# Gates spread by tiny matmuls, an output weight relayed by column tiles, and a head whose weights come in parts

## The chip, the cores and the metric

The kernel runs on one core of one Trainium2 chip. The metric is device time in microseconds (us) of one execution; before the change the median of three runs is 1026.72 us. The core's engines each work through a queue of their own in order: PE (TensorE, matmuls; PEld is its weight load), DVE (VectorE), ACT (ScalarE), POOL (GpSimd), and SP (SyncE), which here issues every DMA transfer.

## The reference, cut to what matters

Two blocks A and B, equal in form and with weights of their own, read the same x (2048 x 640). Each projects q, k, v, splits them into 32 heads of 20 columns and 4 segments of 512 rows, runs causal softmax attention inside each segment, and adds a read from a memory that has been summed over the earlier segments. A gate per row of x mixes the two blocks.

```python
phi = lambda t: jnp.where(t > 0, t + 1.0, jnp.exp(t))
g = _sigmoid(beta).reshape(1, H, 1, 1)                  # per head
for s in range(N):                                      # N = 4 segments of L = 512
    logits = jnp.einsum("bhqd,bhkd->bhqk", qs, ks) * scale + mask
    a_dot = jnp.einsum("bhqk,bhkd->bhqd", _softmax(logits, axis=-1), vs)
    num = jnp.einsum("bhld,bhde->bhle", pq, M)          # pq = phi(qs)
    den = jnp.einsum("bhld,bhd->bhl", pq, z)[..., None] + 1e-6
    outs.append(g * num / den + (1.0 - g) * a_dot)
    M = M + jnp.einsum("bhld,bhle->bhde", pk, vs)       # pk = phi(ks)
    z = z + jnp.einsum("bhld->bhd", pk)
return o @ wo                                           # o: outs, heads joined
...
g = _sigmoid((x * gate_w).sum(-1, keepdims=True))       # per row of x
return g * a + (1 - g) * b
```

## The kernel before, in words

**Windows and quads.** The work is cut into 8 windows, t = 0 to 7: window t is block t % 2 (A or B) of segment t // 2. Each window has 8 quads of 4 heads, 64 quads in all. A quad has three stages on PE. The S units (L1250) multiply q blocks with keys into PSUM banks, and DVE takes the causal row maximum out of each (L1237, with mx). The maxima are cast (mt, L1261, L1262), transposed on PE (L1275), copied by ACT (mr, L1292) and sent by two small DMAs (L1287) into two extra rows of the quad's q tile. The T units (L1340) then make the transposed logits with the maximum already taken off; ACT exponentiates them (p, L1332) and POOL zeroes the part above the diagonal (L1333). The PV unit (L1362, the whole array) multiplies p with the values. L1208 loads a quad's q and k (qst, kst) from DRAM, where L719 had stored them.

**Matmuls by halves.** Numbers are fp32; products are made of a high and a low part (wh, wl; two row tiles for x), three matmuls per k tile. But for the head, the last products and PV, each matmul uses 64 of the array's 128 rows, and two streams of such matmuls, the two "lanes", run beside each other (L737 for all projections). The head (L785) is the first q and k product, 30 full matmuls over the five k tiles of x. L322 are matmuls on zeros, at the start (`WARM`) and between the head's steps (`IDLE_STEPS`).

**What sets the order.** Nothing is scheduled by the hardware or a compiler: the kernel's own Python keeps a clock for each engine and queue, with a cost for each instruction, and writes instructions in the order in which that clock would have them ready. `put(engine, cost, emit, then, prio)` queues an instruction on A(CT), D(VE), G(pSimd) or S(P); `dma(us, emit, then, prio, lat)` queues a transfer on SP; `later(prio, ...)` offers a small PE unit to be slipped between others. The table `RULES` gives, for a quad number, the order of S and T units and four numbers (span, calm, lag, room) that steer how much other work lies between them. Between the units PE is filled with the window's jobs: q, k, v products, the output products of the window before (job o), and the next window's first products. What stands in an engine's queue behind an instruction that waits, waits too.

**Head.** `stage(i)` fetches the weights of job i into a staging tile (wst), ACT casts the high part (L538), DVE or POOL subtracts for the low part (L540); L575, L565 and L569 do the same for a tile of x. For the first two jobs this is one transfer of 320 KB each. `begin` stages some jobs ahead and calls `relay(b)` for block b's wo.

**Gates.** The gate's logit per row of x comes out of the v product as one extra column: ACT copies it into pg (L1055), four columns per segment. `spread(s)` has ACT copy it in 16 pieces into the layout the output needs (pgt, L629), ACT takes the exponential for both signs (L592), and DVE adds one (L593, in `over_sigmoid`). Then POOL multiplies the row gates with the head gates (gq, L660). `head_gates` does the same once for the two betas (L599, L592, L593), right after the head's loads.

**wo's relay.** wo's rows have to be re-ordered by heads before job o can load them. `relay(b)` does it by DMA from DRAM to DRAM in three stages: L481 writes nat (5 transfers), L474 writes lin (4), L469 writes wop (4). All transfers of a stage are queued at once, and a stage begins when the one before has landed. Job o then loads a column tile of wop into wst (L548).

Of the kernel before, what the change touches and what calls it, by code (L numbers as in the profile page):

```python
# [12 lines left out]
F32 = mybir.dt.float32  # L13
# [29 lines left out]
def tile_gated_mix_infini_attn(  # L43
# [47 lines left out]
        0: "TTSTSTSTSS 1.0 2.38 0.31 4",  # L91
        1: "TSTSTSTSTS 1.001 2.38 0.32 6",
        3: "TTSTSTSTSS 1.018 2.38 0.32 6",
        4: "TSTSTTSTSS 0.97 2.38 0.33 3",
        5: "TSSTTSSTTS 1.028 2.94 0.33 8",
        6: "TTTSTSTSSS 1.0 2.14 0.33 6",
        7: "TSTSTSTSTS 1.0 2.69 0.33 6",
        8: "TTSSTTSSTS 1.0 2.1 0.33 6",
        9: "TTSTSTSTSS 1.0 2.38 0.33 6",
        10: "TSTSTSTSTS 1.0 2.38 0.33 6",  # L100
        11: "TSTSTSTSTS 0.964 2.38 0.31 6",
        12: "TSTSTSTSTS 0.932 2.38 0.31 6",
        13: "TTSTSTSTSS 0.949 2.38 0.31 6",
        14: "STSTSTSTST 0.963 2.38 0.31 3",
        15: "STSTSTSTST 0.963 2.38 0.38 3",
        16: "TSTSTSTSTS 1.0 2.38 0.33 6",
        18: "TSTSTSTSTS 0.962 1.59 0.3 8",
        19: "TSTSTSTSTS 1.0 2.38 0.33 6",
        20: "TSSTTSSTTS 1.0 2.38 0.33 6",
        21: "TSSTTSSTTS 1.0 2.38 0.46 6",  # L110
        22: "TSTSTSTSTS 0.999 2.38 0.46 8",
        23: "STTSSTTSST 1.0 2.14 0.33 6",
        24: "TSTSTSTSTS 1.0 2.38 0.33 3",
        25: "TSTSTTSTSS 1.036 2.32 0.42 6",
        26: "STTSSTTSST 1.075 2.08 0.42 6",
        27: "STTSSTTSST 1.0 2.38 0.32 6",
        28: "SSTSTSTSTT 1.0 2.38 0.32 6",
        29: "STTSSTTSST 1.03 1.75 0.32 3",
        30: "TSSTTSSTTS 0.95 2.51 0.42 6",
        31: "STSTSTSTST 0.962 2.51 0.42 6",  # L120
        32: "STSTSTSTST 0.932 2.51 0.32 6",
        33: "TTSSTTSSTS 1.027 2.38 0.33 4",
        34: "TSTSTSTSTS 0.965 2.38 0.33 6",
        35: "TTTSTSTSSS 0.997 2.38 0.33 6",
        36: "TSTSTSTSTS 0.985 3.27 0.33 6",
        38: "TSTSTSTSTS 0.944 3.27 0.33 6",
# [12 lines left out]
        51: "STTSSTTSST 1.002 2.38 0.33 6",
        52: "TTTSTSTSSS 0.994 2.38 0.33 6",  # L140
        53: "TSTSTSTSTS 1.0 2.38 0.3 6",
        54: "TSTSTSTSTS 1.0 1.89 0.46 6",
        56: "TTSSTTSSTS 1.0 2.38 0.33 6",
        57: "TSTSTSTSTS 0.975 1.47 0.33 6",
        59: "SSTSTSTSTT 1.0 2.38 0.3 6",
        60: "TSTSTSTSTS 1.0 2.38 0.31 6",
# [155 lines left out]

    def small_tiles():
# [20 lines left out]
    WARM = 9  # L324
    IDLE_STEPS = {3: 5, 4: 2}
# [25 lines left out]
    pgt = const.tile([P, 16 * NSEG], F32, name="pgt")  # L351
# [59 lines left out]
    ROWS = (slice(0, 64), slice(64, 128))  # L411
# [47 lines left out]

    def relay(b):  # L460
# [7 lines left out]
        def third(j):  # L468
            dma(1.2, lambda: nc.sync.dma_start(  # L469
                out=wop[b][32 * j:32 * j + 32], in_=lin[b][j].rearrange("(k q) c -> q k c", k=KT)), last, prio=RELAY[b])  # L470

        def second():
            for j in range(4):
                dma(1.2, lambda j=j: nc.sync.dma_start(  # L474
                    out=lin[b][j].rearrange("(u e) c -> u e c", e=DH),
                    in_=nat[b].rearrange("(u j e) c -> j u e c", u=8, j=4)[j]), lambda j=j: third(j), prio=RELAY[b])

        last = then_all(4, there)
        first = then_all(KT, second)
        for m in range(KT):  # L480
            dma(1.2, lambda m=m: nc.sync.dma_start(  # L481
                out=nat[b][:, P * m:P * (m + 1)].rearrange("(k p) c -> p k c", p=P), in_=weights[b]["o"][m]), first, prio=RELAY[b])
# [3 lines left out]
    VK = ((0, 2), (2, 4), (4, 5))  # L486
    staged = set()
    split = {}

    def stage(i):  # L490
# [35 lines left out]

        def got(w):
# [18 lines left out]
            def fetch():  # L546
                src_ = src[m] if kind in "qk" else wop[t % 2][:, :, P * m:P * (m + 1)]
# [7 lines left out]
        wst.want(1, got, prio=i)  # L555
# [34 lines left out]
    def over_sigmoid(out, in_, sign):  # L590

        nc.scalar.activation(out, in_, AF.Exp, scale=-sign)  # L592
        nc.vector.tensor_scalar(out, out, 1.0, None, op0=ALU.add)  # L593

    def head_gates():
# [4 lines left out]

        def over():
            for b in range(2):
                over_sigmoid(gmem[b], gsel[b], 1.0)
                over_sigmoid(gdot[b], gsel[b], -1.0)

        put("D", 0.8, over, prio=6)
# [18 lines left out]
    def spread(s):  # L625

        def some(a):
            for j in range(4):
                nc.scalar.copy(  # L629
                    pgt[32 * j:32 * j + 32, 16 * s + a:16 * s + 16:4], pg[32 * a:32 * a + 32, NB * s:NB * (s + 1)])  # L630

        def over():
            put("D", 0.5, lambda: segment_gate(s), lambda: (gates_ready.add(s), ask_gates()), prio=7)

        left = then_all(4, over)
        for a in range(4):
            put("A", 0.44, lambda a=a: some(a), left, prio=5)

    def segment_gate(s):
        c = slice(16 * s, 16 * (s + 1))  # L640
        for b, sign in ((0, 1.0), (1, -1.0)):
            over_sigmoid(gate[b][:, c], pgt[:, c], sign)
# [123 lines left out]
    def job_head():  # L766
# [3 lines left out]
        while todo:  # L770
            ready_ = [x for x in todo if x[1] in split and (0, x[0]) in xs]
# [861 lines left out]
```

## Time and profile before

| what | value |
|---|---|
| median of 3 runs | 1026.72 us (1025.70 to 1028.92) |
| the profiled execution: its time, its span | 1025.48 us, 1023.8 us |
| granted TensorE clock | 0.999 |
| busy: PE, DVE, POOL, ACT | 1011.4, 742.7, 735.7, 645.8 us |
| DMA: moved, mean rate | 212 MB, 207 GB/s |

How to read it: PE's busy time counts a moment as busy when either lane works, so a lane that stands alone does not show there. A row of the timeline is: start, length, engine, line, operation, tiles, and in brackets the engine's idle time before it with what ended it. A row of the waits is: who waited for whom, the total in us, how often, the longest. A row of the windows is: the stretch, its length, then for each engine the busy us and the number of instructions, then the granted clock, the DMA engines' share and GB/s.

### The profile page before, as it was taken

The page shows a single profiled execution, that of the slowest core. Times are in us where ns is not written, and L with a number is a line of the kernel's source. Part 1 is how long each engine was busy: PE and PEld are TensorE (multiplying, and loading weights), DVE is VectorE, ACT ScalarE, POOL GpSimd, SP SyncE. Part 2 cuts the span into 40 slices and gives each one's busy share as a digit, 9 for nine tenths or more (in the row PEclk, how much of TensorE's full clock was granted, in tenths as well). Part 3 has the DMA queues.
Part 4 walks back from the last instruction along what each step waited for, and adds up shares of the span by engine and source line. Part 5 has one row for each costly group of instructions (what it writes and reads, how often), then busy time and mean ns, then how long its engine had stood idle before and what let it go on. Part 6 is the DMA issues. An engine that isn't in the chain of part 4 may idle for free.

```text
span 1023.8 us, 29705 instructions
## 1 busy us (share of the span) xinstructions
PE 1011.4 (99%) x10612; PEld 843.4 (82%) x10612; DVE 742.7 (73%) x2570; ACT 645.8 (63%) x1420; POOL 735.7 (72%) x1375
## 2 busy tenths in 40 slices
PE   8999999999999999999999999999999999999998
PEld 7988888888788988888877888888878798887885
DVE  4687876678677678676688668786677776878853
ACT  6576666567755476665876547666486556657672
POOL 4565867767486786976858679697686956868684
PEclk9999999999999999999999999999999999999999
DMA  7998988758556666755766457585665766776522
GB/s 257 277 298 259 318 275 297 222 170 259 149 182 179 190 221 188 245 160 151 276 179 215 136 181 235 165 252 152 184 215 176 247 192 198 237 201 204 157 91 99
DMA packets 136158, 212.09 MB, mean 207 GB/s; under 512 B 12549, under 2 KB 48650, under 8 KB 135946
## 3 DMA queue, kind: packets, MB, share of 16 engines
q1 hardware_dynamic: 136010, 210.19, 66.8%
q8 instruction: 84, 1.38, 0.6%
q14 instruction: 64, 0.52, 0.2%
HBM read 135.69 MB, written 83.23 MB: 214 GB/s over the span
## 4 chain that ended last, share of the span: by engine, by line
PE 91%; ACT 3%; DMA 3%; DVE 1%; issue 1%; SPq 0%; POOL 0%; ACTq 0%
PE bank L737 54%; PE bank L1362 13%; PE bank L1340 7%; PE bank L1250 7%; PE bank L830 4%; PE bank L1002 3%; DMA row<-in_xT_dram 1%; ACT p L1332 1%; PE bank L963 1%; DMA kst<-kd 1%; PE bank L785 1%; DMA qst<-mr 1%; ACT pgt L629 0%; PE bank L1179 0%; DVE row L1164 0%
## 5 line engine op out<-in xcount | busy, mean ns | idle before, releaser
L1237 DVE CUSTOM_DVE_ANT_0 bank<-bank,tri 128x384 f32<-128x384 f32 (+3 forms) x1024 | 473.7, 516 | 103.6 <-PE bank L1250 85.7
L737 PE MATMUL bank<-row,wh 64*128 64x512 f32 x2308 | 526.5, 405 | 0.1
L1332 ACT ACTIVATE p<-bank 128x512 f32<-128x512 f32 x538 | 297.6, 601 | 142.7 <-PE bank L1340 109.5
L737 PEld LDWEIGHTS bank<-row,wh 64*128 64x128 f32 x2308 | 328.8, 185 | 19.2 <-issue 3.2
L737 PE MATMUL bank<-row,wl 64*128 64x512 f32 x1154 | 312.7, 399 | 0.0
L1333 POOL TENSOR_SCALAR_AFFINE_SELECT p<-p 128x256 f32<-128x256 f32 (+1 forms) x538 | 193.6, 370 | 97.0 <-ACT p L1332 87.6
L737 PE MATMUL bank<-wvh,row 64*128 64x320 f32 (+1 forms) x1280 | 204.8, 316 | 0.1
L540 POOL TENSOR_TENSOR wl<-wst,wh 128x640 fp32r<-128x640 f32 x115 | 179.5, 1565 | 31.7 <-ACT wh L538 31.1
L737 PEld LDWEIGHTS bank<-row,wl 64*128 64x128 f32 x1154 | 179.8, 185 | 6.5 <-issue 0.8
L1340 PE MATMUL bank<-qst,kst 62*128 62x512 f32 (+3 forms) x1024 | 177.1, 323 | 4.1 <-DVE mx L1237 1.5
L1250 PE MATMUL bank<-kst,qst 60*128 60x384 f32 (+3 forms) x1024 | 176.8, 318 | 1.2 <-ACT p L1332 0.6
L737 PEld LDWEIGHTS bank<-wvh,row 64*128 64x128 f32 x1280 | 164.5, 186 | 4.8 <-issue 1.7
L940 DVE STREAM_TRANSPOSE row<-bank 128x512 f32<-128x512 f32 x112 | 78.1, 707 | 98.8 <-PE bank L1362 71.4
L1362 PE MATMUL bank<-p,vst 128*32 128x384 f32 (+3 forms) x1804 | 144.9, 423 | 0.0
L1237 DVE DVE_READ_ACCUMULATOR2_ANT mx<- 128x1 f32 x1024 | 144.4, 141 | 0.0
L1340 PEld LDWEIGHTS bank<-qst,kst 62*128 62x128 f32 x1024 | 129.9, 186 | 17.3 <-issue 5.1
L1250 PEld LDWEIGHTS bank<-kst,qst 60*128 60x128 f32 x1024 | 130.3, 186 | 12.0 <-issue 2.3
L1362 PEld LDWEIGHTS bank<-p,vst 128*32 128x32 f32 x1804 | 57.7, 110 | 79.7 <-issue 57.0
L737 PE MATMUL bank<-wvl,row 64*128 64x320 f32 (+1 forms) x640 | 117.6, 313 | 0.0
L538 ACT CAST wh<-wst 128x640 fp32r<-128x640 f32 x119 | 86.6, 740 | 32.5 <-PE bank L737 14.8
L737 PEld LDWEIGHTS bank<-wvl,row 64*128 64x128 f32 x640 | 91.4, 186 | 0.5 <-issue 0.2
L1332 ACT ACTIVATE row<-bank 128x512 f32<-128x512 f32 x102 | 56.8, 601 | 52.7 <-PE bank L1340 48.4
(100 smaller groups left out, 1311.5 us busy)
## 6 DMA issues: line engine op xcount, KB each, us to landing
qd<-row SPq DMA_DIRECT2D x120, 256.0 KB
kd<-row SPq DMA_DIRECT2D x120, 256.0 KB
qst<-qd SPq DMA_DIRECT2D x128, 240.0 KB
kst<-kd SPq DMA_DIRECT2D x128, 240.0 KB
wst<-wop SPq DMA_DIRECT2D x40, 320.0 KB
wst<-in_a_wq_dram SPq DMA_DIRECT2D x20, 320.0 KB
wst<-in_a_wk_dram SPq DMA_DIRECT2D x20, 320.0 KB
wst<-in_b_wq_dram SPq DMA_DIRECT2D x20, 320.0 KB
```

Source lines behind the costliest of these rows:

```text
L538: put("A", 0.628, lambda: nc.scalar.copy(wh, w3), lambda: put(lo_eng, lo_cost, lambda: lo.tensor_tensor(out=wl, in0=w3, in1=r32(wh), op=AL ...
L540: lambda: lo.tensor_tensor(out=wl, in0=w3, in1=r32(wh), op=ALU.subtract), end, prio=3), prio=6)
L737: return nc.tensor.matmul(bank_of, lhsT=w[ROWS[half]], rhs=x_[ROWS[half]], start=start, stop=stop)
L830: return nc.tensor.matmul(b, lhsT=w[r], rhs=r32(pqTs[t, half_m[half]][r, :]), start=start, stop=stop)
L940: put("D", 0.635, lambda: nc.vector.transpose(out=z, in_=b), turned, prio=2)
L1002: return nc.tensor.matmul(b[:, :nh * E1], lhsT=r32(pkn[ROWS[half], P * n:P * (n + 1)]), rhs=vst[ROWS[half], n, LO[m] * E1:(HI[m] + 1) * E1 ...
L1237: put("D", w / 960.0 + 0.112, lambda: nc.vector.tensor_tensor_reduce(out=sc[:, off:off + w], in0=sc[:, off:off + w], in1=tri[:, L - w:], s ...
L1250: lane_ops[half].append((cost_r(w), lambda pair=pair, qb=qb, off=off, w=w, r=r, sc=sc: nc.tensor.matmul(sc[:, off:off + w], lhsT=q[r, pair ...
L1332: put("A", 0.493, lambda: nc.scalar.activation(pt, sc, AF.Exp, scale=SCALE), lambda: (bank.give(sc), put("G", 0.156 + 0.118 * len(todo), l ...
L1333: "G", 0.156 + 0.118 * len(todo), lambda: nc.gpsimd.affine_select(out=blocks, in_=blocks, pattern=[[0, len(todo)], [1, P]], base=0, channe ...
L1340: lane_ops[half].append((cost_r(w), lambda pair=pair, kb=kb, off=off, w=w, r=r, sc=sc: nc.tensor.matmul(sc[:, off:off + w], lhsT=k[r, pair ...
L1362: nc.tensor.matmul(po[32 * j:32 * j + 32, P * kb:], lhsT=vst[:, kb, h * E1:h * E1 + 32], rhs=pts[i, n, f][0][:, off:off + w], start=(kb == ...
```

## The change

- **Gates.** `spread` becomes a PE unit: four matmuls of 64 x 128 by 64 x 4 with a 0/1 matrix `pick`, two on each half of the array, spread pg's columns over the partitions in a PSUM bank. ACT takes exponential and adds one (`nc.scalar.add`), for both signs: four ACT instructions per segment. The 16 copies and the two DVE additions per segment go. `head_gates` has its additions on ACT too, and its two loads are asked for when job 4 begins, no longer ahead of the head's end. POOL makes `pick` once with four copies.
- **wo's relay.** nat, lin and wop are laid out by column tiles of 128. The last stage has 20 transfers of 80 KB in place of 4 of 400 KB, and a helper `in_turn` keeps two transfers of the first and second stage and four of the third on the way at a time. A column tile of wop is now contiguous for job o's load.
- **Head.** The first two jobs' weights come, and are split, in two parts (k tiles 0 and 1, then 2 to 4). The head takes a step once its part is there. `WARM` goes from 9 to 7, and the `IDLE_STEPS` (7 matmuls on zeros) go.
- **Order.** The planner's cost of a DMA's issue goes from 0.37 to 0.48 (0.66 in the relay, 0.7 for L1287's), and `RULES` is another table; the order of all instructions follows from these.

```diff
-        0: "TTSTSTSTSS 1.0 2.38 0.31 4",
-        1: "TSTSTSTSTS 1.001 2.38 0.32 6",
...
+        0: "TSTSTSTSTS 0.97 1.02 0.33 6",
+        1: "TSTSTSTSTS 0.958 1.0 0.46 6",
...
-    def dma(us, emit, then=None, prio=5, lat=2.4, some=False):
+    def dma(us, emit, then=None, prio=5, lat=2.4, some=False, iss=0.48):
...
-        put("S", 0.37, emit, issued, prio)
+        put("S", iss, emit, issued, prio)
...
+        for half in range(2):
+            for c in range(2):
+                nc.gpsimd.tensor_copy(
+                    out=pick[ROWS[half], c, :].rearrange("p (j r) -> p j r", r=32),
+                    in_=ident[ROWS[half], None, 64 * half + 32 * c:64 * half + 32 * c + 32].to_broadcast([64, 4, 32]))
...
-    WARM = 9
-    IDLE_STEPS = {3: 5, 4: 2}
+    WARM = 7
...
+    def in_turn(todo, width, then):
+        left = then_all(len(todo), then)
+        todo = deque(todo)
+
+        def one():
+            if todo:
+                us, emit, prio = todo.popleft()
+                dma(us, emit, lambda: (one(), left()), prio=prio, iss=0.66)
+
+        for _ in range(width):
+            one()
...
+        prio = RELAY[b]
+        in_turn([(1.1, lambda m=m: first(m), prio) for m in range(KT)], 2, lambda: in_turn(
+            [(1.3, lambda j=j: second(j), prio) for j in range(4)], 2, lambda: in_turn(
+                [(0.3, lambda m=m, j=j: third(m, j), prio) for m in range(KT) for j in range(4)], 4, there)))
...
+    HEAD_K = ((0, 2), (2, KT))
...
-        nc.vector.tensor_scalar(out, out, 1.0, None, op0=ALU.add)
+        nc.scalar.add(out, out, 1.0)
...
     def spread(s):
-        def some(a):
-            for j in range(4):
-                nc.scalar.copy(
-                    pgt[32 * j:32 * j + 32, 16 * s + a:16 * s + 16:4], pg[32 * a:32 * a + 32, NB * s:NB * (s + 1)])
...
+        b = bank.free.pop(0)
+        ops = [[((LOAD, 0.06, 0.06), lambda a, z, half=half, c=c: nc.tensor.matmul(
+            b[:, 2 * half + c:16:4], lhsT=pick[ROWS[half], c, :], rhs=pg[ROWS[half], NB * s:NB * (s + 1)],
+            start=True, stop=True)) for c in range(2)] for half in range(2)]
...
+        def segment_gate():
+            c = slice(16 * s, 16 * (s + 1))
+            for g, sign in zip(gate, (1.0, -1.0)):
+                over_sigmoid(g[:, c], b[:, :16], sign)
+
+        return split_unit(*ops, lambda: put("A", 0.85, segment_gate, there, prio=3))
...
-            ready_ = [x for x in todo if x[1] in split and (0, x[0]) in xs]
+            ready_ = [x for x in todo if x[::-1] in head_there and (0, x[0]) in xs]
...
-        gates_in = then_all(NB, lambda: spread(t // 2))
+        gates_in = then_all(NB, lambda: later(2, 0.2, lambda: True, lambda: spread(t // 2)))
```

How the order of instructions moves, at three places. First SP's queue at the very start, before and after: wst are the weights' staging tiles, row the tiles of x.

```order
L548 DMA wst_123<-in_a_wq_dram 128x640
L575 DMA row_9_172<-in_xT_dram 128x512
L548 DMA wst_124<-in_a_wk_dram 128x640
L575 DMA row_16_175<-in_xT_dram 128x512
L575 DMA row_21_178<-in_xT_dram 128x512
L575 DMA row_26_181<-in_xT_dram 128x512
L575 DMA row_31_184<-in_xT_dram 128x512
L548 DMA wst_125<-in_a_wq_dram 128x640
L548 DMA wst_126<-in_a_wk_dram 128x640
L1552 DMA beta_185<-in_a_beta_dram 128x32
L1552 DMA beta_186<-in_b_beta_dram 128x32
L522 DMA wst_123<-in_a_wv_dram 128x640
```

```order
L572 DMA wst_131<-in_a_wq_dram 128x256
L625 DMA row_12_182<-in_xT_dram 128x512
L572 DMA wst_132<-in_a_wk_dram 128x256
L625 DMA row_18_185<-in_xT_dram 128x512
L572 DMA wst_131<-in_a_wq_dram 128x384
L572 DMA wst_132<-in_a_wk_dram 128x384
L625 DMA row_25_188<-in_xT_dram 128x512
L625 DMA row_30_191<-in_xT_dram 128x512
L625 DMA row_35_194<-in_xT_dram 128x512
L598 DMA wst_133<-in_a_wq_dram 128x640
L598 DMA wst_134<-in_a_wk_dram 128x640
L1587 DMA gw<-in_gate_w_dram 5x128
```

The second tile of x stands behind 384 KB less of weights and the third behind none less; the loads of beta are gone from here.

Second the gates of segment 1. On DVE before, the two additions stand between the row maxima of two quads:

```order
L1237 ISA bank_116,mx_4402<-bank_116,tri 128x128
L1237 ISA mx_4402 128x1
L593 TENSOR_SCALAR gate_81<-gate_81 128x16
L593 TENSOR_SCALAR gate_82<-gate_82 128x16
L1237 ISA bank_122,mx_4402<-bank_122,tri 128x512
L1237 ISA mx_4402 128x1
```

On ACT after, where all of the gate's elementwise work now is:

```order
L1096 COPY pg<-bank_130 128x1
L1097 COPY vst<-bank_130 128x16x20
L1373 ACTIVATE p_5441_4524<-bank_127 128x512
L1373 ACTIVATE p_5440_4523<-bank_129 128x512
L1373 ACTIVATE p_5498_4562<-bank_125 128x512
L1373 ACTIVATE p_5499_4563<-bank_123 128x512
L642 ACTIVATE gate_81<-bank_127 128x16
L643 ACTIVATE gate_81<-gate_81 128x16
L642 ACTIVATE gate_82<-bank_127 128x16
L643 ACTIVATE gate_82<-gate_82 128x16
L531 CAST wvh<-wst_133 128x2x320
```

And on PE after, where the first half's two tiny matmuls stand among projections and S units:

```order
L781 MATMUL bank_126<-row_3259_2766,wh_137 128x512
L672 MATMUL bank_127<-pg,pick 128x4 x2
L781 MATMUL bank_126<-row_3264_2769,wh_137 128x512
L781 MATMUL bank_129<-row_3253_2762,wh_139 128x512
L781 MATMUL bank_126<-row_3269_2772,wh_137 128x512
L1291 MATMUL bank_125<-kst_77,qst_73 128x384
```

DVE has nothing left to do for the gates; PE now has a row that needs ACT's copy of pg (L1096), with four exponentials on ACT after the last copy and ahead of the gate itself.

Third SP's queue inside block B's relay, before and after:

```order
L1287 DMA qst_72<-mr_144 2x8x128 x2
L548 DMA wst_123<-wop_113 128x5x128
L522 DMA wst_126<-in_b_wv_dram 128x640
L522 DMA wst_124<-in_b_wv_dram 128x640
L522 DMA wst_125<-in_b_wv_dram 128x320
L474 DMA lin_112<-nat_110 8x12800 x4
L1208 DMA qst_75<-qd_90 60x2x512 x2
L1208 DMA kst_79<-kd_98 60x2x512 x2
L469 DMA wop_114<-lin_112 160x1x640
```

```order
L1249 DMA kst_79<-kd_98 60x2x512 x2
L493 DMA wop_4_117<-lin_111 160x1x128
L488 DMA lin_112<-nat_110 40x2560
L763 DMA kd_98<-row_3111_2660 128x512 x2
L763 DMA kd_98<-row_3112_2661 128x512
L763 DMA qd_90<-row_3124_2666 128x512
L1328 DMA qst_73<-mr_153 2x8x128 x2
L763 DMA qd_90<-row_3124_2666 128x512
L763 DMA qd_90<-row_3125_2667 128x512
L598 DMA wst_133<-wop_0_113 128x640
```

Four transfers of 400 KB stood together ahead of a quad's loads; now one stands alone, and block A's last third-stage transfer lies eight rows ahead of the first load of its wop.

More of the change, by code (lines that the diff above doesn't have):

```diff
@@ L103, in tile_gated_mix_infini_attn @@
[L103 to L114, printed above, removed]
@@ L350, in tile_gated_mix_infini_attn @@
     pg = const.tile([P, NSEG * NB], F32, name="pg")
-    pgt = const.tile([P, 16 * NSEG], F32, name="pgt")
+    pick = const.tile([P, 2, P], F32, name="pick")
     qd = [dram.tile([D, 3, L], F32R, name=f"qd{i}") for i in range(8)]
@@ L356, in tile_gated_mix_infini_attn @@
     part = [dram.tile([D, L], F32, name=f"part{s}") for s in range(NSEG)]
-    nat = [dram.tile([D, D], F32, name=f"nat{b}") for b in range(2)]
-    lin = [dram.tile([4, 8 * DH, D], F32, name=f"lin{b}") for b in range(2)]
-    wop = [dram.tile([P, KT, D], F32, name=f"wop{b}") for b in range(2)]
+    nat = [dram.tile([KT, D, P], F32, name=f"nat{b}") for b in range(2)]
+    lin = [dram.tile([4, KT, 8 * DH, P], F32, name=f"lin{b}") for b in range(2)]
+    wop = [[dram.tile([P, KT, P], F32, name=f"wop{b}_{m}") for m in range(KT)] for b in range(2)]
     NBIG, NWST, NWH, SPARE = 42, 4, 4, 2
@@ L466, in there, with first, second, third @@
                 x[1]()
[L468 to L472, printed above, removed]
-            for j in range(4):
[L474 to L482, printed above, removed]
+        def first(m):
+            nc.sync.dma_start(out=nat[b][m].rearrange("(k p) c -> p k c", p=P), in_=weights[b]["o"][m])
+        def second(j):
+            nc.sync.dma_start(
+                out=lin[b][j].rearrange("m (u e) c -> (m u) (e c)", e=DH),
+                in_=nat[b].rearrange("m (u j e) c -> j (m u) (e c)", u=8, j=4)[j])
+        def third(m, j):
+            nc.sync.dma_start(
+                out=wop[b][m][32 * j:32 * j + 32], in_=lin[b][j][m].rearrange("(k q) c -> q k c", k=KT))
+        prio = RELAY[b]
+        in_turn([(1.1, lambda m=m: first(m), prio) for m in range(KT)], 2, lambda: in_turn(
+            [(1.3, lambda j=j: second(j), prio) for j in range(4)], 2, lambda: in_turn(
+                [(0.3, lambda m=m, j=j: third(m, j), prio) for m in range(KT) for j in range(4)], 4, there)))
     RELAY = (150.0, 260.0)
     VK = ((0, 2), (2, 4), (4, 5))
+    HEAD_K = ((0, 2), (2, KT))
+    head_pair, head_parts, head_there = {}, {}, set()
     staged = set()
@@ L525, in stage, with got_head, take, end @@
             return
+        def got_head(w):
+            w3 = w.rearrange("p (k n) -> p k n", n=P)
+            def take(pair):
+                head_pair[i] = pair
+                def end():
+                    wst.give(w)
+                    split[i] = pair
+                done = then_all(len(HEAD_K), end)
+                for a, b in HEAD_K:
+                    head_parts[a, i] = lambda a=a, b=b: part_(a, b, pair, done)
+            def part_(a, b, pair, done):
+                wh, wl = (x[:, a:b, :] for x in pair)
+                def landed():
+                    put("A", 0.1 + 0.106 * (b - a), lambda: nc.scalar.copy(wh, w3[:, a:b, :]), lambda: put(
+                        "D", 0.06 + 0.155 * (b - a), lambda: nc.vector.tensor_tensor(
+                            out=wl, in0=w3[:, a:b, :], in1=r32(wh), op=ALU.subtract), over, prio=3), prio=6)
+                def over():
+                    head_there.update((i, k) for k in range(a, b))
+                    done()
+                dma(0.185 * (b - a), lambda: nc.sync.dma_start(
+                    out=w3[:, a:b, :], in_=weights[t % 2][kind][m][:, a:b, :]), landed, prio=0)
+            whl.want(1, take, prio=i)
         def got(w):
```

146 lines of the change are left out of this document (77 added, 69 removed).

## The prediction

> **What bounds the kernel now.** First the page's busy line, the shares of the chain that ended last, and then the windows, to see where PE stands still.
>
> ```profile
> PE 1011.4 (99%) x10612; PEld 843.4 (82%) x10612; DVE 742.7 (73%) x2570; ACT 645.8 (63%) x1420; POOL 735.7 (72%) x1375
> PE 91%; ACT 3%; DMA 3%; DVE 1%; issue 1%; SPq 0%; POOL 0%; ACTq 0%
> 0.00:10.00 10.00, 7.41 (x22) 4.85 (x22) 3.29 (x5) 4.55 (x6) 7.38 (x18) 1.00 0.77 249
> 100.00:107.00 7.00, 5.91 (x63) 3.71 (x63) 5.09 (x18) 1.96 (x5) 5.74 (x10) 1.00 0.80 292
> 160.00:180.00 20.00, 19.41 (x229) 17.41 (x227) 12.69 (x49) 13.63 (x28) 15.28 (x28) 1.00 0.91 295
> 270.00:280.00 10.00, 8.08 (x61) 5.24 (x58) 7.49 (x20) 8.57 (x25) 5.02 (x11) 1.00 0.43 144
> 400.00:500.00 100.00, 100.00 (x1070) 85.26 (x1071) 69.67 (x245) 64.22 (x136) 78.37 (x141) 1.00 0.62 188
> 530.00:540.00 10.00, 9.59 (x100) 6.70 (x96) 7.33 (x26) 9.19 (x32) 5.73 (x11) 1.00 0.63 197
> 540.00:550.00 10.00, 9.30 (x74) 6.53 (x67) 9.41 (x29) 6.03 (x15) 8.47 (x14) 1.00 0.73 246
> 1010.00:1024.00 14.00, 9.66 (x49) 7.54 (x47) 5.56 (x10) 0.62 (x1) 2.90 (x3) 0.92 0.25 94
> ```
>
> PE is the bound: 91% of the chain, 100.00 of 100 us busy in an undisturbed stretch. So only two things can shorten the run: less on PE, or fewer places where PE starves. PE's idle time is 1023.8 - 1011.4 = 12.4 us. Of it 2.6 lie in the first 10 us, 4.1 after 1010 (13.8 - 9.66), and the rest in few spots: 1.1 at 100 to 107, 0.6 at 160 to 180, 1.9 at 270 to 280, 1.1 at 530 to 550. A lane that stands alone counts as busy, so the true loss is larger, and the number of matmuls bounds it: the undisturbed stretch does 10.7 per us, 270 to 280 does 61, which is 5.7 us' worth: up to 4.3 us lost. 540 to 550 with 74 lost up to 3.1, 530 to 540 with 100 up to 0.7. These are upper ends, since long matmuls make the count small too.
>
> Next the waits and the chain, for what PE waited on in those spots.
>
> ```profile
> DVE gate L593 <- ACT gate L592: 3.4, 3, 2.0
> PE bank L1340 <- DVE mx L1237: 1.5, 1, 1.5
> PE bank L1340 <- DMA qst<-mr: 1.1, 1, 1.1
> ACT pg L1055 <- PE bank L737: 13.0, 6, 4.3
> SPq L719 <- DMA lin<-nat: 7.3, 5, 2.3
> 99.60 6.14 DMA qst<-mr
> ```
>
> ```profile
> 275.24 1.56 POOL L540 TENSOR_TENSOR wl<-wst,wh 128x640 fp32r<-128x640 f32 x1 [0.36 <-ACT wh L538]
> 275.31 1.60 DVE L593 TENSOR_SCALAR gate<-gate 128x16 f32<-128x16 f32 x2 [1.24 <-ACT gate L592]
> 277.62 0.50 PE L1340 MATMUL bank<-qst,kst 62*128 62x512 f32 x2 [1.49 <-DVE mx L1237]
> 539.02 1.47 DVE L593 TENSOR_SCALAR gate<-gate 128x16 f32<-128x16 f32 x2 [2.04 <-ACT gate L592]
> ```
>
> The spots at 270 and 540 are the gates of segments 1 and 2. DVE reaches L593, waits 1.24 and 2.04 us for ACT's exponential, and then needs 1.60 and 1.47 us for two additions of 16 columns, ending with the POOL subtraction that began beside it. Row maxima stand behind it, and PE's next L1340 waits 1.49 us. The spot at 100 is a transfer of 8 KB (qst<-mr) that took 6.14 us to land while wo's relay was on the way; SP's queue, too, waited 7.3 us for lin's transfers.
>
> **The change part by part.**
>
> *Head.* The rows of the start:
>
> ```profile
> 1.52 3.80 PE L322 MATMUL bank<-qst 128*128 128x512 f32 x9 [1.52 <-DVE qst L316]
> 2.18 6.60 DMA row<-in_xT_dram
> 6.51 1.31 PE L322 MATMUL bank<-qst 128*128 128x512 f32 x5
> 9.47 0.50 PE L785 MATMUL bank<-row,wh 128*128 128x512 f32 x1 [0.94 <-ACT row L565]
> 9.47 5.66 PE bank L785 x22
> 11.56 1.54 ACT L538 CAST wh<-wst 128x640 fp32r<-128x640 f32 x2 [0.18 <-DMA wst<-in_a_wq_dram]
> 13.01 1.70 ACT L599 COPY betaq<-beta 32x8 f32<-32x8 f32 x8
> 15.93 0.50 PE L737 MATMUL bank<-row,wh 64*128 64x512 f32 x1
> ```
>
> PE does 6 of the 30 steps and then starves for x's second tile until 9.47; the rest runs at 5.66 / 22 = 0.257 us a step. Now that tile stands behind 384 KB less, about 1.5 us at the first window's 249 GB/s, so 12 steps are done when the third tile arrives: 6 x 0.257 = 1.5 us saved if the third lands when the second did. It stands behind as much as before, so it may land up to 1 us later; on the other side the next weights' cast, at 11.56, allows products from 12.4 on, 3.5 us earlier than 15.93. ACT's beta copies (1.70 us) no longer stand ahead of the value weights' cast. I take -1.8, near the 1.5, with ends -3.5 and -0.5. The removed matmuls on zeros cost nothing now, they fill the waits for x (0.94 us of it idle); the first 9 still end before the first step. Two more transfers on SP delay the next weights by under 1 us, hidden by the same 12 steps. POOL's four copies for pick stand ahead of the masks that the first DVE maxima need, some 20 us later.
>
> *Gates.* ACT's 16 copies per segment and both DVE additions go; two short ACT instructions come in.
>
> ```profile
> L629 ACT COPY pgt<-pg x64: 180/195/199, 36.6 to 787.9; 32x4 f32<-32x4 f32 x64
> L593 DVE TENSOR_SCALAR gate<-gate x8: 163/304/1518, 40.6 to 791.5; 128x16 f32<-128x16 f32 x8
> L861 ACT ACTIVATE fw<-row x48: 221/232/262, 287.6 to 951.4; 128x16 f32<-128x16 f32 x48
> 19.53 0.43 PE L963 MATMUL bank<-ident,row 64*128 64x64 f32 x4
> L963 PE MATMUL bank<-ident,row 64*128 64x64 f32 x240 | 25.9, 226 | 0.0
> L612 PE MATMUL bank<-ident,gw 64*128 64x64 f32 x2 | 0.5, 271 | 0.0
> ```
>
> ACT loses 64 x 0.195 = 12.5 us and gains 8 x 0.232 = 1.9 (L861 is the same form); it is busy 63%, so neither counts by itself. What counts is DVE's blocked queue: it disappears, since DVE has no gate row any more. Worth between the array's idle time there, 1.9 + 1.1 = 3.0 us, and the counts' 4.3 + 3.1 + 0.7 = 8.1. I take -5.0, nearer the idle time, because the lower counts also hold the long matmuls of the memory reads. Added on PE: 16 matmuls with a weight load of 128 columns, like L963's; four of those take 0.43 us, so they follow at (0.43 - 0.23) / 3 = 0.07, where 0.23 is the mean length of one. 16 x 0.07 = 1.1, half of it beside the other lane: +0.6; ends 0 and 16 x 0.27 = 4.3, if each stood alone as L612's do (0.27). New wait: PE's tiny matmuls need ACT's copy of pg, and behind them stands all of PE. ACT's row for that copy waits for PE (13.0 us in 6), not the other way, so ACT takes pg as soon as the product ends: 0 for it, with a rival below.
>
> *Relay.* Same bytes in smaller and fewer transfers at a time. PE lost 1.1 us at 104 and 0.6 at 173, both in the relays: -1.7, with ends -2.0 and +1.0. SP issues 32 transfers more, 0.593 us each by this row:
>
> ```profile
> L469 SPq DMA_DIRECT2D wop<-lin x8: 567/593/1434, 106.7 to 178.7; - x8
> L548 SPq DMA_DIRECT2D wst<-wop x40: 529/570/812, 143.7 to 985.2; - x40
> ```
>
> That is 19 us of SP over more than 100 us, between transfers that wait for their own engines; hidden unless the relay comes late (rival). The Trainium skill, "DMA: Bandwidth & Descriptors", § Bandwidth, says the opposite of what is done here: batch transfers, to 1 MiB where possible, since each has a fixed cost of about 2 us. By it 32 more transfers, four at a time, would make the two relays 16 us longer in all, and the sum would stay, as nothing waits for them within that time.
>
> *Order.* The table moves every unit. Nothing in the trace of before prices that. Counted over both orders, neighbouring matmuls on the same half of the array, which leave the other lane alone, fall from 1392 to 1315; that speaks for a small gain. I take -1.0; ends -4.0 and +3.0, about what the dips in the undisturbed windows could give or take.
>
> *Sum.* -1.8 - 5.0 + 0.6 - 1.7 - 1.0 = -8.9 against the profiled execution's 1025.48: 1016.6. The median of the runs is 1026.72, 1.24 above that execution, so 1017.8.
>
> **The rivals.**
>
> *The waits only move.* What DVE's block hid comes up behind it: at 540 DVE is busy 9.41 of 10 us even so, at 270 ACT 8.57, and either would be the next to be late. Then the gates give the idle time of one spot, 2.0, and the order nothing: -1.8 - 2.0 + 0.6 - 1.7 = -4.9, median 1021.8. Against it: ACT loses 16 x 0.195 = 3.1 us of copies in just that stretch.
>
> *Slower: the relay comes late.* The last stage needs 20 / 4 = 5 rounds, and each waits for landings, at the lowest priority on SP. Before, the first wop transfer was issued at 106.7 and its first reader at 143.7: 37 us. Five rounds fit if one takes under 7.4 us. With landings of 6.14 us as at 99.60 plus the issue behind other transfers it is close; at 9 us a round wo comes 8 us late, SP stands at the load of wop with the quads' loads behind it, and PE stands with it: -8.9 + 2 x 8 = +7.1, median 1034. Against it: fewer bytes on the way at a time should make landings shorter.
>
> *A cold array.* The nine first matmuls took 3.80 us, 0.42 each, the five at 6.51 about 0.24 once the length of the last is taken off: PE began at about half its speed, though the windows grant it 1.00. With 7 warm-ups and no idle steps the head could run slow: 30 steps x (0.42 - 0.23) = 5.7 us, so -8.9 + 5.7 = -3.2, median 1023.5. The Trainium skill, "TensorE: Matmul & The Clock Gate", § Part 1: The HAM clock gate, says so: the array starts at half clock and needs about 3.4 us of sustained activity, and an idle window puts it back. Against the rival: 7 x 0.42 = 2.9 us of warm-up and 12 steps of the head follow each other with less idle time than before, and x's third tile bounds those 12 steps anyway.
>
> *The order is worth more.* With the lower ends of head, gates, and order, -3.5 - 6.5 + 0.6 - 1.7 - 4.0 = -15.1, median 1011.6 and below.
>
> **How the numbers follow.** Chances: forecast 0.62, waits only move 0.17, order worth more 0.09, slower 0.08, cold array 0.04. 0.3% of 1026.72 is 3.1 us, about what a measurement can tell from no change, so faster means below 1023.6. The forecast and the fourth case are faster, 0.71, and two thirds of the second, 0.11: 0.82. The rest of the second and the cold array: same, 0.10. Slower 0.08. The range takes the forecast, most of the fourth case and all of the second: 1009.5 to 1025.5.
>
> **What would show it.** Head right: L737's row begins at 13 to 14.5 us in place of 15.93, and PE is busy over 8.5 of the first 10 us. Gates right: no DVE wait for a gate, and no stretch of 10 us around the gates with PE under 9.7 busy. Relay right: no landing above 4 us of an 8 KB transfer between 60 and 180, and PE idle there under 0.5 us. The forecast is wrong if the windows between the old spots show new dips of 1 us and more, if PE's waits name ACT's pg or a DMA from wop, or if the first L826 rows follow at 0.4 us.

## The result, and the profile after

The changed kernel takes 1010.58 us (median of 4 runs, 1009.80 to 1012.97) against 1026.21 (4 runs) for the kernel before: ratio 0.9848, 95% interval 0.9821 to 0.9876, or 15.6 us less. The forecast was 1017.8 with 1009.5 to 1025.5. The profiled execution took 1012.97 us, the slowest of the four; its span is 1011.3.

First the page's busy line, the shares of the chain and the windows of the spots that the prediction named (columns as before: stretch, length, PE, PEld, DVE, ACT, POOL with counts, granted clock, DMA share, GB/s).

```profile
PE 1001.1 (99%) x10637; PEld 835.3 (83%) x10637; DVE 737.8 (73%) x2558; ACT 640.9 (63%) x1372; POOL 734.8 (73%) x1379
PE 96%; DMA 2%; SPq 1%; DVE 0%; issue 0%; ACT 0%; ACTq 0%
0.00:10.00 10.00, 7.57 (x20) 5.23 (x21) 4.08 (x8) 4.87 (x8) 8.41 (x22) 1.00 0.76 222
100.00:107.00 7.00, 7.00 (x83) 5.82 (x83) 5.85 (x19) 5.95 (x13) 5.94 (x14) 1.00 0.77 286
160.00:180.00 20.00, 19.87 (x242) 17.39 (x239) 12.79 (x47) 16.00 (x32) 15.29 (x25) 1.00 0.96 319
270.00:280.00 10.00, 9.91 (x74) 7.40 (x70) 5.11 (x16) 5.40 (x16) 6.61 (x13) 1.00 0.62 166
540.00:550.00 10.00, 9.93 (x94) 8.87 (x92) 8.19 (x26) 5.21 (x14) 8.06 (x21) 1.00 0.33 115
```

The spots at 104, 270 and 540 are filled; the one at 170 nearly. What PE waits for now, in its waits (who for whom, total us, times, longest; the first is the start and was 1.5 before, too):

```profile
PE bank L328 <- DVE qst L322: 1.5, 1, 1.5
PE bank L1291 <- DVE row L1020: 1.1, 1, 1.1
PE bank L826 <- ACT row L615: 0.9, 2, 0.6
PE bank L657 <- DMA gw<-in_gate_w_dram: 0.8, 1, 0.8
PE bank L1381 <- ACT p L1373: 0.8, 1, 0.8
PE bank L1381 <- DMA qst<-mr: 0.2, 1, 0.2
```

No wait names the gates any more. But PE's idle time explains little of the result: it falls from 12.4 us to 1011.3 - 1001.1 = 10.2. PE is *busy* 10.3 us less, with 25 matmuls more in its records (32 rows of the tiny ones come in, 7 on zeros go). So the gain lies in stretches that count as busy; that a lane stood alone there is the reading, and the counts of matmuls agree with it. A window without gates, relay or head shows it, 600 to 700, first of before and then of after:

```profile
600.00:700.00 100.00, 99.87 (x1054) 81.96 (x1052) 80.64 (x272) 65.55 (x139) 80.61 (x145) 1.00 0.68 209
```

```profile
600.00:700.00 100.00, 100.00 (x1089) 83.48 (x1087) 78.58 (x260) 69.12 (x147) 81.04 (x148) 1.00 0.69 214
```

Both are full, yet the second does 35 matmuls more in the same 100 us. It is the widest gap of the six windows from 300 to 900, which hold 6335 and 6452 matmuls together. To see where the time was won, take one event per quad, the first row of its PV unit in PE's timeline (start, length, line). Quads 12, 28, 44 and 60 of before, then of after:

```profile
231.40 0.62 PE L1362 MATMUL bank<-row,vst 128*32 128x512 f32 x2
...
495.38 1.06 PE L1362 MATMUL bank<-p,vst 128*32 128x512 f32 x8
...
752.46 0.62 PE L1362 MATMUL bank<-row,vst 128*32 128x512 f32 x2
...
976.70 0.62 PE L1362 MATMUL bank<-p,vst 128*32 128x512 f32 x2
```

```profile
232.90 0.62 PE L1403 MATMUL bank<-row,vst 128*32 128x512 f32 x2
...
487.77 1.06 PE L1403 MATMUL bank<-row,vst 128*32 128x512 f32 x8
...
741.20 1.06 PE L1403 MATMUL bank<-p,vst 128*32 128x512 f32 x8
...
962.97 1.07 PE L1403 MATMUL bank<-p,vst 128*32 128x512 f32 x8
```

The differences are +1.5, -7.6, -11.3, -13.7 us. At quad 12 head and both relays are over, and this execution had gained nothing; the gain grows from there to near the end, through gates and quiet stretches alike. Two things limit the reading. The execution had stray waits of 0.8 us at 153 and 1.1 at 180; the kernel with whole head weights (below), whose order is otherwise the same, was profiled at 1010.47 us and has the four events at 230.13, 485.06, 738.38 and 960.34, that is 1.3, 10.3, 14.1 and 16.4 us ahead of the kernel before. And single quads scatter by some us (-7.4 at quad 48, -17.3 at quad 56), since a rule moves a unit against the work around it; only the trend counts.

One correction to the text ahead of the prediction: `IDLE_STEPS` names 7 matmuls, but only the five after step 3 are issued, so the change removes 2 + 5 matmuls on zeros, not 2 + 7 (PE has 14 rows of them before, 7 after).

### The profile page after: what moved, and what is told of

The parts are those of the page before. It is cut to its first block, busy times and chain, and to the rows that moved or that the text cites. A ratio compares the mean times of both kernels' runs of the same rounds, so it can differ in the third digit from the quotient of the medians.

```text
span 1011.3 us, 29724 instructions
## 1 busy us (share of the span) xinstructions
PE 1001.1 (99%) x10637; PEld 835.3 (83%) x10637; DVE 737.8 (73%) x2558; ACT 640.9 (63%) x1372; POOL 734.8 (73%) x1379
## 4 chain that ended last, share of the span: by engine, by line
PE 96%; DMA 2%; SPq 1%; DVE 0%; issue 0%; ACT 0%; ACTq 0%
PE bank L781 57%; PE bank L1403 15%; PE bank L1381 7%; PE bank L1291 7%; PE bank L871 4%; PE bank L1043 3%; PE bank L1004 1%; DMA gw<-in_gate_w_dram 1%; DMA kd<-row 1%; DMA qst<-mr 1%; PE bank L1316 0%; PE bank L1220 0%; DVE row L1205 0%; PE bank L826 0%; SPq L625 0%
## 5 line engine op out<-in xcount | busy, mean ns | idle before, releaser
L1278 DVE CUSTOM_DVE_ANT_0 bank<-bank,tri 128x256 f32<-128x256 f32 (+3 forms) x1024 | 475.1, 515 | 116.5 <-PE bank L1291 101.4
L781 PE MATMUL bank<-row,wh 64*128 64x512 f32 x2308 | 525.7, 405 | 0.1
L781 PEld LDWEIGHTS bank<-row,wh 64*128 64x128 f32 x2308 | 325.6, 185 | 18.1 <-PE bank L781 2.9
L781 PE MATMUL bank<-row,wl 64*128 64x512 f32 x1154 | 311.8, 400 | 0.0
L781 PE MATMUL bank<-wvh,row 64*128 64x320 f32 (+1 forms) x1280 | 199.9, 317 | 0.1
L781 PEld LDWEIGHTS bank<-row,wl 64*128 64x128 f32 x1154 | 178.6, 185 | 7.3 <-issue 1.2
L1381 PE MATMUL bank<-qst,kst 62*128 62x384 f32 (+3 forms) x1024 | 176.2, 321 | 0.9 <-ACT p L1373 0.8
L781 PEld LDWEIGHTS bank<-wvh,row 64*128 64x128 f32 x1280 | 160.9, 186 | 2.8 <-PE bank L781 0.9
L1403 PE MATMUL bank<-p,vst 128*32 128x384 f32 (+3 forms) x1828 | 142.5, 423 | 0.0
L781 PE MATMUL bank<-wvl,row 64*128 64x320 f32 (+1 forms) x640 | 115.9, 314 | 0.0
L781 PEld LDWEIGHTS bank<-wvl,row 64*128 64x128 f32 x640 | 90.2, 186 | 0.9 <-issue 0.8
L871 PE MATMUL bank<-row,mall 64*128 64x512 f32 x192 | 81.6, 602 | 0.0
```

The lines of the kernel that those rows point to most:

```text
L781: return nc.tensor.matmul(bank_of, lhsT=w[ROWS[half]], rhs=x_[ROWS[half]], start=start, stop=stop)
L871: return nc.tensor.matmul(b, lhsT=w[r], rhs=r32(pqTs[t, half_m[half]][r, :]), start=start, stop=stop)
L1278: put("D", w / 960.0 + 0.112, lambda: nc.vector.tensor_tensor_reduce(out=sc[:, off:off + w], in0=sc[:, off:off + w], in1=tri[:, L - w:], s ...
L1381: lane_ops[half].append((cost_r(w), lambda pair=pair, kb=kb, off=off, w=w, r=r, sc=sc: nc.tensor.matmul(sc[:, off:off + w], lhsT=k[r, pair ...
L1403: nc.tensor.matmul(po[32 * j:32 * j + 32, P * kb:], lhsT=vst[:, kb, h * E1:h * E1 + 32], rhs=pts[i, n, f][0][:, off:off + w], start=(kb == ...
```

## The experiments

**Theory:** most of the gain is the order that the new table gives, fitted to the changed code; the changed instructions give a few us. **Rival:** the gates' additions, the relay and the head carry it, and the table hardly matters.

### The gates' additions alone

On the code before, only the engine of the additions is changed, everything else stays in the same order; on the changed code the same is undone.

```diff
-        nc.vector.tensor_scalar(out, out, 1.0, None, op0=ALU.add)
+        nc.scalar.add(out, out, 1.0)
```

> The kernel before, with one line changed: the gates' additions run on ACT; every other instruction stays where it was in its queue. Theory A (DVE's blocked queue cost a few us at two gates, the rest of the gain is the new order): 3 to 6 us faster than before, about 1021 us, with the idle time of PE at 270 to 280 and 530 to 550 gone and no change elsewhere. Rival B (the blocked queue throws the whole order behind it out of step, so most of the 15.6 us hang on it): 9 us faster or more, below 1017 us. Rival C (the waits only move): within 1.5 us of before.

Measured: 1024.19 us beside 1026.12, ratio 0.9982 (0.9972 to 0.9992), 1.9 us less. That lies between the theory's 3 to 6 us and the 1.5 of the rival that the waits only move. Its windows at the gates, then PE's wait for ACT's p at 540 in the kernel before, and the same line in this run, where the longest is the one at 540:

```profile
270.00:280.00 10.00, 9.35 (x77) 6.24 (x78) 6.73 (x22) 9.74 (x29) 5.19 (x12) 1.00 0.43 151
540.00:550.00 10.00, 8.93 (x68) 6.16 (x66) 9.41 (x28) 6.33 (x15) 8.24 (x14) 1.00 0.72 243
```

```profile
PE bank L1250 <- ACT p L1332: 0.6, 1, 0.6
```

```profile
PE bank L1250 <- ACT p L1332: 1.3, 2, 1.1
```

At 270 PE gains 1.3 us of busy time and its wait of 1.5 us for DVE's maxima is gone; three waits of 0.2 us stay, two of them for ACT's p, and ACT is full now (9.74 of 10). At 540 PE stands as before (8.93, was 9.30), and not because the wait moved: from 530 to 552 its waits named ACT's p already in the kernel before (0.6 and 0.4 us), none DVE's maxima, and with the additions on ACT the first becomes 1.1.

> The changed kernel with the gates' additions back on DVE, in the place in its queue that the planner's time gives, everything else the same. Theory A: the blocked queue of DVE comes back at segments 1 to 3, 3 to 6 us slower than the changed kernel, about 1015 us. Rival B: 9 us or more slower. Rival C (the tiny matmuls, not the additions' engine, made the difference, since the gate is now done early enough): within 1.5 us of the changed kernel.

Measured: 1011.52 us, 0.9 above the changed kernel, inside the changed kernel's spread. DVE's additions again take up to 981 ns and DVE waits 3.5 us for ACT's exponentials, in three places, yet nothing behind them is late:

```profile
L643 DVE TENSOR_SCALAR gate<-gate x8: 160/168/981, 43.0 to 778.0; 128x16 f32<-128x16 f32 x8
```

So the additions are worth 1.9 us in the old order and at most about 1 in the new.

### Tables exchanged

Each code with the other's `RULES`, nothing else changed.

> The code before with the table of the changed kernel. The table sets the order only together with the planner's costs. Theory A (the table and the costs fit each other; a table fitted to other code is worth no more than any): 0 to 8 us slower than before, 1026 to 1034 us. Rival (the new table is better in itself): 5 us faster or more, below 1021 us.

> The changed code with the table of before. Theory A (gates, relay and head bring about 6 us, the rest comes from a table fitted to the new costs): 1017 to 1024 us. Rival (the code alone carries the gain, the table is neutral): 1009 to 1014 us. Rival (a table that does not fit loses all of it): 1026 us or more.

Measured: the code before with the new table 1037.03 us, ratio 1.0106 (1.0086 to 1.0127); the changed code with the old table 1046.16, ratio 1.0194 (1.0174 to 1.0213). Neither table is better by itself: by the exchange the code before loses 10.9 us and the changed code 35.6. Both lose more than the theory had it (0 to 8 us, and a time of 1017 to 1024); the second is the case of the rival that a table that does not fit loses all of the gain. The changed code without its own table is 20 us slower than the kernel before. To part code and fit, both codes need a table that was made for neither.

### One plain rule for both

```diff
-        0: "TSTSTSTSTS 0.97 1.02 0.33 6",
-        1: "TSTSTSTSTS 0.958 1.0 0.46 6",
...
+    RULES = {0: "TSTSTSTSTS 1.0 2.38 0.33 6"}
```

> The code before with one rule for all quads (row 0 of the changed table's plain values: TSTSTSTSTS 1.0 2.38 0.33 6) in place of its fitted table. Theory 'a table fits one code': without a fitted table the kernel loses as the changed code lost with the old table (+20 to the time before): 1040 to 1060 us. Rival 'the table before was hardly fitted': 1024 to 1032.

> The changed code with the same single rule. Theory 'the code parts give a few us and the fitted table the rest': 0 to 6 us below the run with the code before under the same rule, so some 1036 to 1058. Rival 'the code parts carry the gain': 10 us or more below it. Rival 'all is the table': within 3 us of it or above it. Two orders of one code can differ by some us by chance, so a difference below 5 us says only that the code is not the main part.

Measured: before 1056.69 us, ratio 1.0294 (1.0274 to 1.0315); changed 1038.91, ratio 1.0128 (1.0111 to 1.0145). The changed code is 17.8 us ahead, which the theory did not expect (0 to 6) and the rival that the code carries the gain did (10 or more). The first rows of quad 8's PV unit show where, in the code before and in the changed code:

```profile
198.80 1.06 PE L1305 MATMUL bank<-p,vst 128*32 128x512 f32 x8
```

```profile
175.02 1.07 PE L1347 MATMUL bank<-p,vst 128*32 128x512 f32 x8
```

All of it, 23.8 us, arises ahead of quad 8; from there to the end (spans 1055.3 and 1037.0) the changed code loses 5.5 of it again. Windows of the code before in that place, with one of the changed code under the same rule behind them:

```profile
155.00:160.00 5.00, 2.89 (x22) 2.44 (x19) 2.48 (x4) 3.63 (x7) 3.76 (x4) 0.77 0.60 207
...
165.00:170.00 5.00, 2.58 (x14) 1.53 (x14) 3.24 (x6) 2.20 (x5) 2.01 (x3) 0.80 1.03 281
170.00:175.00 5.00, 3.00 (x19) 1.90 (x20) 4.79 (x21) 0.00 (x0) 0.00 (x0) 0.50 0.99 344
```

```profile
160.00:180.00 20.00, 20.00 (x240) 17.45 (x238) 12.21 (x39) 14.63 (x30) 16.29 (x22) 1.00 0.93 322
```

PE's four longest waits in the code before, and three pieces of its chain of waits (start, length, what):

```profile
PE bank L1283 <- DMA qst<-mr: 2.7, 1, 2.7
PE bank L906 <- DVE row L633: 2.2, 1, 2.2
PE bank L945 <- ACT row L922: 2.1, 1, 2.1
PE bank L1305 <- DVE mx L1180: 2.0, 1, 2.0
```

```profile
137.22 2.29 PE bank L1305 x32
...
162.98 6.40 DMA kst<-kd
...
174.21 4.31 PE bank L1305 x32
```

The first of these waits lies at 103, inside block A's relay, for a transfer of 8 KB that took 7.62 us to land; the other three lie between 155 and 175. There the DMA engines are full (1.03 and 0.99 from 165 on), a quad's k needs 6.40 us to land, PE starves, and the granted clock, down to 0.77 at 155 to 160 already, falls to 0.50, so that the same 32 matmuls take 4.31 us in place of 2.29. The changed code is at 20.00 of 20 us busy from 160 to 180 under the same rule. What brings this stall about is open. The old relay's own transfers are not beside it: the last of them was issued at 146.4 us, and from 155 to 172 SP issues only stores and loads of q and k and two loads of the finished wop. Whether the relay had pushed these together is not shown: the plain rule without the relay was not run.

### The relay left out

In both kernels the relay's transfers are left out and job o loads wo's tiles as they are, so the re-ordering of wo's rows is missing; the order of everything else is kept.

```diff
-            nc.sync.dma_start(out=nat[b][m].rearrange("(k p) c -> p k c", p=P), in_=weights[b]["o"][m])
+            skip(out=nat[b][m].rearrange("(k p) c -> p k c", p=P), in_=weights[b]["o"][m])
...
-                src_ = src[m] if kind in "qk" else wop[t % 2][m]
+                src_ = src[m]
```

> The changed kernel with the relay's transfers left out (job o loads wo's tiles unsorted, so the re-ordering of wo's rows is not done); the order of everything else is kept. Theory 'the relay costs next to nothing now': 0 to 2.0 us below the changed kernel (its idle spots at 153 and 180 hold 1.9 us), so 1009 to 1011. Rival 'smaller and more transfers still slow the loads beside them': 3 us or more below, under 1007.6.

> The kernel before with the relay's transfers left out in the same way. By the prediction's term the relay cost 1.7 us (1.1 at 104 and 0.6 at 173): 1023.5 to 1025.5. Theory 'the relay's spots were hidden behind later waits': within 0.7 us of the kernel before. Rival 'long transfers cost more than the idle time shows': 3 us or more below, under 1023.

Measured: changed code 1010.13 us, 0.45 below the changed kernel; code before 1022.11, ratio 0.9965 (0.9951 to 0.9979), 3.2 below its neighbour. In the tuned orders the old relay cost about 3.2 us (2.2 to 5.0 by the interval), the new one 0.5 or nothing (against the kernel before that was measured beside each, both ratios are 0.9848), so its change is worth some 2.7. In the second kernel the two spots at 100 and 160 are gone and the gates' are not:

```profile
100.00:107.00 7.00, 7.00 (x80) 4.58 (x77) 6.15 (x23) 3.33 (x8) 6.70 (x15) 1.00 0.95 318
160.00:180.00 20.00, 20.00 (x241) 18.39 (x239) 13.71 (x54) 15.29 (x31) 16.44 (x28) 1.00 0.79 271
270.00:280.00 10.00, 8.27 (x76) 4.62 (x76) 8.01 (x21) 8.65 (x22) 6.53 (x12) 1.00 0.49 128
```

### Each table up to quad 9, then the plain rule

```diff
         9: "TTSSTTSSTS 1.073 1.44 0.33 8",
-        10: "TTTSTSTSSS 1.073 1.44 0.3 8",
...
+        10: "TSTSTSTSTS 1.0 2.38 0.33 6",
     }
```

> The code before with its own rules for quads 0 to 9 and the single plain rule from quad 10 on. Theory 'the table before gives little behind the relays': the loss under the plain rule from the eighth quad on was 76.1 us against 68.3 with the table, so about +8: 1030 to 1037 us. Rival 'both tables give the same behind quad 9': the loss is as large as the changed code's in the run beside it.

> The changed code with its own rules for quads 0 to 9 and the same plain rule from quad 10 on. Theory 'the gain over the kernel before lies in the rules from quad 10 on': the loss there was 80.3 us under the plain rule against 56.5 with the table, so about +24: 1028 to 1038, that is, level with the run beside it within 6 us. Rival 'the changed instructions carry the gain': still 10 us or more below the run beside it.

Measured: code before 1032.78 us, ratio 1.0061 (1.0048 to 1.0073); changed code 1027.41, ratio 1.0011 (1.0002 to 1.0021). So the rules from quad 10 on are worth 1032.78 - 1026.01 = 6.8 us to the code before and 1027.41 - 1010.58 = 16.8 to the changed code. The difference, 10.0 us, is about two thirds of the gain; the other 5.4 are the changed instructions, the planner's costs and the first rules together. With the plain rule from quad 10 on, the changed code's events at quads 12, 28, 44 and 60 come 4.2, 1.0, 2.5 and 4.3 us ahead of the other run's: behind quad 12 it gains nothing more without its own rules. The share of the rules still depends on the rule that is taken as neutral; one plain rule for all quads gave 17.8 us between the codes. The window of 600 to 700, seen again in these two runs:

```profile
600.00:700.00 100.00, 99.63 (x1029) 82.37 (x1028) 76.47 (x256) 67.02 (x140) 79.41 (x141) 1.00 0.68 205
```

```profile
600.00:700.00 100.00, 100.00 (x1044) 84.23 (x1043) 77.47 (x257) 64.73 (x138) 78.10 (x143) 1.00 0.67 205
```

With the plain rule the changed code does 1044 matmuls there, below the 1054 of the kernel before; its own rules bring 1089. So the changed instructions, which lie elsewhere, are not what fills this stretch.

### The head

```diff
+                    if i == 0 and a > 0:
+                        nc.sync.dma_start(out=gw[:KT], in_=gate_w.rearrange("(k p) -> k p", p=P))
                     nc.sync.dma_start(out=w3[:, a:b, :], in_=weights[t % 2][kind][m][:, a:b, :])
```

> The changed kernel with the load of gate_w issued ahead of the head's second weight part; the order on all other queues is kept. Theory 'the head's gain went into the wait for gate_w': PE's 0.84 us wait at L657 goes and L781 begins at about 14.8, total 0.5 to 0.9 below: 1009.7 to 1010.2. Rival 'work behind the head absorbs it': within 0.3 of the changed kernel. Rival 'the load delays the weights': 0.3 to 1 above.

```diff
-                    out=w3[:, a:b, :], in_=weights[t % 2][kind][m][:, a:b, :]), landed, prio=0)
+                    out=w3, in_=weights[t % 2][kind][m]) if a == 0 else None, landed, prio=0)
```

> The changed kernel with each of the head's two weights in one transfer, as before; the casts stay in two parts, the order on the other engines is kept. By the prediction's term the parts saved 1.5 us: 1012.1. Theory 'the wait only moved from x's second tile to its third': the second waits about 1 us longer, the third less; L781 begins within 0.5 of 15.65 and the total is within 0.5: 1010.1 to 1011.1.

Measured: 1010.59 us with gate_w's load ahead, 1010.34 with the weights whole, against 1010.58. Neither moves the time. PE's timeline of the changed kernel, then of the kernel with whole weights, then of the one with the early load (in brackets the idle time before the row):

```profile
9.72 0.50 PE L826 MATMUL bank<-row,wh 128*128 128x512 f32 x1 [0.55 <-ACT row L615]
...
12.96 0.24 PE L657 MATMUL bank<-ident,gw 64*128 64x64 f32 x1 [0.84 <-DMA gw<-in_gate_w_dram]
...
15.65 0.50 PE L781 MATMUL bank<-row,wh 64*128 64x512 f32 x1
```

```profile
8.94 0.50 PE L826 MATMUL bank<-row,wh 128*128 128x512 f32 x1 [0.89 <-ACT row L615]
...
15.53 0.50 PE L781 MATMUL bank<-row,wh 64*128 64x512 f32 x1
```

```profile
10.11 0.50 PE L830 MATMUL bank<-row,wh 128*128 128x512 f32 x1 [1.08 <-ACT row L619]
...
15.15 0.50 PE L785 MATMUL bank<-row,wh 64*128 64x512 f32 x1
```

The head waits once for x whatever the weights do: for the second tile when they come whole, for the third when they come in parts. The early load removes the 0.84 us wait, gives half of it back at x's third tile (1.08 in place of 0.55) and starts L785 (L781 in the other two) 0.5 us sooner, and even that is not in the total.

## Why the prediction was right, and where its sum was not

The direction and the range held, and the likeliest case did not: 1010.58 is the rival *the order is worth more* (1011.6 "and below", chance 0.09). That the time lies in the range, and so near this rival, is luck in part: the sum had -8.5 from head, gates and relay, of which the runs show about 4, and -1.0 from the order, where they show 10; the rival's own sum took 3.5 from the head and 6.5 from the gates (not the lower end that it names, which is 8.1) and only 4.0 from the order. By its terms:

- **Order, -1.0 (ends -4.0 and +3.0): the step that failed.** The rules from quad 10 on alone brought 10 us more to the changed code than to the one before. The sentence behind it, "only two things can shorten the run: less on PE, or fewer places where PE starves", was taken from a window 100.00 busy, and the ends from the visible dips. The prediction had said itself that a lone lane counts as busy, but priced that only at the spots with idle time. The window of 600 to 700 holds the loss: full in both, 1054 matmuls against 1089, or 35 / 10.7 = 3.3 us in that stretch alone; from 300 to 900 it is 117 / 10.7 = 10.9 us, an estimate, since long and short matmuls count alike. The neighbours on one half of the array, 1392 to 1315, pointed the right way and were not turned into time.
- **Gates, -5.0 (ends -3.0 and -8.1): the mechanism was half right.** DVE's block went and PE's busy time at 270 and 540 rose to 9.91 and 9.93, as foretold. But the additions alone are worth 1.9 us, and undoing them in the new order costs 0.9. At 540 the prediction took DVE's block for PE's wait, where PE's waits name ACT's p. ACT, without its 16 copies per segment, is busy 6.91 us from 530 to 540 in place of 9.19, which may be what filled that spot; what the copies and the new order share of it was not parted.
- **Tiny matmuls, +0.6: counted too few, and never priced by a run.** PE has 32 rows at L672, two for each of the 16, so by its own working the term is 32 x 0.07 / 2 = +1.1. No wait of PE names pg; it is ACT that waits 0.69 us for L672 at 270.
- **Relay, -1.7 (ends -2.0 and +1.0): right in kind, small in size.** Left out, it shows -2.7. *The relay comes late* did not happen. The Trainium skill, "DMA: Bandwidth & Descriptors", § Bandwidth, would have larger transfers; here the relay with 20 of 80 KB, four at a time, cost 0.5 us or nothing, the one with 4 of 400 KB 3.2. Layout, size and number on the way changed together, so which of them did it is not shown. The small loads did not all land sooner: one of 8 KB, from 110.48, still took 5.23 us, where the prediction had named none above 4 as its sign, but PE waited only 0.2 us for it. The claim that PE would be idle under 0.5 us in the relays failed in the profiled execution, with 0.8 for ACT's p and 1.1 for DVE's row L1020; the chain puts the second down to a store of k that took 6.54 us to land. The run with whole head weights shows neither of the two, but one of 0.7 for ACT's mr between 170 and 180, so such waits change from run to run. The prediction had named new dips of 1 us as a sign against it; the one at 180 reaches that.
- **Head, -1.8 (ends -3.5 and -0.5): wrong.** L781 began at 15.65, not at 13 to 14.5, and PE was busy 7.57 of the first 10 us, not 8.5. The failed step is "if the third lands when the second did": PE had it at 9.72 in place of 9.47, and gate_w's load, now behind more transfers, added a wait of 0.84 us that the prediction had not looked for. With the weights whole the total is 1010.34, so the parts were worth nothing.
- **A cold array: slow rows, without a price.** Rows at 0.4 us were a sign against the forecast, and they came. These are the first rows of the head in the changed kernel:

```profile
5.24 0.79 PE L826 MATMUL bank<-row,wh 128*128 128x512 f32 x1 [0.36 <-ACT row L615]
5.83 0.63 PE L826 MATMUL bank<-row,wl 128*128 128x512 f32 x1
6.25 1.05 PE L826 MATMUL bank<-row,wh 128*128 128x512 f32 x2
7.11 0.43 PE L826 MATMUL bank<-row,wl 128*128 128x512 f32 x1
7.38 0.62 PE L826 MATMUL bank<-row,wh 128*128 128x512 f32 x2
```

The first four follow at (7.11 - 5.24) / 4 = 0.47 us, from 7.11 on at about 0.25: some 0.9 us lost, but ahead of the 0.55 us wait for x's third tile, which would only have been longer without it.

The parts add up roughly: 10.0 for the later rules, 2.7 for the relay, 1 to 2 for the additions, 0 for the head make 13.7 to 14.7 of 15.6. They are not independent, as the plain rule shows, where the changed code won 23.8 us by quad 8: the old table's order does not have that stall, so part of what it is worth lies there. Open is whether a table fitted anew to the old code would have brought the 10 us too, which planner cost or rule brings them, and what the stall under the plain rule is due to.

## What to carry to other kernels

A stretch at 100% busy may still hold the largest gain, when two streams share an engine: compare the number of instructions per us between windows, or when the same event starts, before pricing the order at next to nothing. A fitted order belongs to one code; judge a code change under a rule that was fitted to neither version, and cut the table at a point to see from where on it earns. A wait removed from one engine is worth only the distance to the next engine in line, which a version with that one edit shows; and a blocked engine beside a dip is not yet what PE waited for.

## What of the hardware was not expected

**The clock after a stall.** Under the plain rule the granted clock was 0.77 from 155 to 160, 0.80 from 165 to 170, 0.50 from 170 to 175, 0.68 from 175 to 180, and 1.00 only behind 190; the PV unit took 4.31 us against 2.29. The Trainium skill, "TensorE: Matmul & The Clock Gate", § Part 1: The HAM clock gate, puts the array back to half clock after an idle window of about 3.4 us; the trace agrees on the half, but PE's longest single wait in this run was 2.7 us, and those from 155 to 175 were 2.0 to 2.2. So a stall costs more than its idle time.

**Two additions of 16 columns.** They took 1518 ns at most in before and 163 at least, and 981 at most when put back. The long ones of before ended with POOL's subtractions of 1.56 and 1.44 us that ran beside them. The Trainium skill, "SBUF — State Buffer", § SBUF: two separate sides, tells of a port pair that POOL and some DVE instructions lock for a whole instruction; the 1518 ns fit that. What surprised is how little it cost: 1 to 2 us of the whole.
